# One pool of eight one-bank PSUM tiles for the last group of a DeltaNet and maxout kernel

## The chip, the cores and the metric

The kernel runs on one core of one Trainium2 chip. The metric is the time of one execution on the device, in microseconds (us); the time of a kernel is the median of several runs.

## The reference

The first half is a DeltaNet recurrence over 4 batches, 8 heads, 768 steps and 48 dimensions. The second half is a maxout layer on its 3,072 tokens, 384 wide, with 768 hidden units. All is float32.

```python
for t in range(S):
    y[:, :, t] = einsum('bhd,bhde->bhe', q[:, :, t], state)
    v_old = einsum('bhde,bhd->bhe', state, kt)
    state = state + bt[:, :, :, None] * einsum('bhd,bhe->bhde', kt, vt - v_old)
...
h = maximum(maximum(x @ w1, x @ w2), x @ w3)
out = h @ w_out
```

## The kernel before, in words

The sequence is cut into chunks of 64 steps, and two chunks of all batches make a group of 512 tokens; there are six groups. The order of all instructions is written out by hand: the loop at L1427 steps through the generator `ffn(m)`, which is the layer of group m, and between two of its yields issues pieces of the recurrence of group m + 1. The last group (m = 5) has no recurrence beside it, so from its first instruction on only the layer runs.

Every matmul writes into PSUM, which has eight banks. The pool `psum` (L76) hands them out under two tags. `ps_ffn` (L80) gives a tile of one bank and has 2 buffers. `ps_two` (L83) gives a tile of two banks and has 3 buffers, so the eight banks are all in use. When a tile is asked for and the buffers of its tag are all taken, the matmul that writes it waits until the reader of the buffer that comes free first is done.

The layer of the last group is worked out in two parts.

- **`crossed_hidden` (L1067)** makes the hidden values. Its two halves of 256 tokens, two of its three blocks of 128 inputs and pairs of 128 hidden units form a 2 by 2 by 2 block product, which is done with seven block products instead of eight (Strassen's scheme in Winograd's form), and the third block of inputs is added on top. Before the first product VectorE (DVE) makes four sums of the tokens, s1 to s4 (L1083 to L1086). Then come six units, for three pairs of hidden blocks and, for each, the second and the third weight (the first has been subtracted out of both, so the maximum is taken with zero and the first weight's part is added later). A unit has eight products, each in its own PSUM tile, `bank(0)` to `bank(7)`, and eleven matmuls of 128 by 256. Since a float32 matmul is two instructions on TensorE (PE), that is 22 per unit, 132 for the six. Products 0, 2, 3 and 4 are copied out of PSUM by ScalarE (ACT) into m1, m7, m5 and m6 (L1121, L1127, L1130, L1134). DVE makes four sums of these (L1135 to L1138) and adds the products 1, 5, 6 and 7 to them straight out of PSUM (`result`, L1108). In every second unit each of the four is followed by the maximum with the hidden values (L1110).
- **`outputs` (L947)**, used for the last two groups, makes the output in the same way. It takes two one-bank tiles, p and q, once, and uses them by turns: eleven products of twelve instructions of 128 by 192 each, 132 in all (L960). Its last instruction that reads PSUM is the DVE addition at L1042, which reads p; the addition at L1038 is the last that reads q. The helper `op` (L989) records all of these.

In `bank(n)` (L1114) the odd products take a `ps_ffn` tile and the even ones the first bank of a `ps_two` tile, whose second bank stays unused. So five products at most are in PSUM at once, three even and two odd. The tiles are named p_e and p_c in the profile, and those of `outputs` p_o.

Of the kernel before, what the change touches and what calls it, by code (L numbers as in the profile page):

```python
# [9 lines left out]
FP32 = mybir.dt.float32  # L10
# [13 lines left out]
def kernel(  # L24
# [42 lines left out]
    TOK = 512  # L67
# [5 lines left out]
    dram = ctx.enter_context(  # L73
        tc.tile_pool(name="dram", bufs=2, space=bass.MemoryType.DRAM)
    )
    psum = ctx.enter_context(  # L76
        tc.tile_pool(name="psum", bufs=1, space=bass.MemoryType.PSUM)
    )

    def ps_ffn(shape, name):  # L80
        return psum.tile(shape, FP32, name=name, tag="ffn", bufs=2)

    def ps_two(name):  # L83
        return psum.tile([128, 2, 512], FP32, name=name, tag="two", bufs=3)


    kpad = [const.tile([128, H, DP], FP32, name=f"kpad{i}") for i in range(4)]
# [21 lines left out]
    def rows(bb):  # L109
        return slice(C * bb, C * (bb + 1))  # L110
# [196 lines left out]
    def square(name):  # L307
        return work.tile([128, H, C], FP32, name=name, tag="square", bufs=17)
# [758 lines left out]
    def crossed_hidden(m, hs):  # L1067


        xt, vec = xts[m], nc.vector.tensor_tensor  # L1070
        plus = vec if m == GROUPS - 1 else nc.gpsimd.tensor_tensor
        lo, hi = slice(0, 256), slice(256, 512)
        a11, a12, a13 = (xt[:, t, lo] for t in range(KT))
        a21, a22, a23 = (xt[:, t, hi] for t in range(KT))
        spare = [t.rearrange("p a h d -> p (a h d)") for t in kmore]
        s1, s2, s3, s4 = (spare[0][:, 256 * n : 256 * (n + 1)] for n in range(4))
        parts = [
            work.tile([128, 2, HB * BL + HB], FP32, name=name, bufs=1).rearrange(
                "p s r -> p (s r)"
            )  # L1080
            for name in ("x_bl", "y_bl")
        ]
        vec(out=s3, in0=a11, in1=a21, op=ALU.subtract)  # L1083
        vec(out=s1, in0=a21, in1=a22, op=ALU.add)
        vec(out=s2, in0=s1, in1=a11, op=ALU.subtract)
        vec(out=s4, in0=a12, in1=s2, op=ALU.subtract)  # L1086
        for j in range(FT):
            hs[j] = square("h").rearrange("p h c -> p (h c)")
        for unit in range(2 * PAIRS):
            j, i = divmod(unit, 2)  # L1090
            w = {
                name: t[:, 128 * j : 128 * (j + 1)]
                for name, t in thirds[1 + i].items()
            }
            top, bottom = hs[j], hs[j + PAIRS]
            held = parts[unit % 2]
            m1, m5, m6, m7 = (held[:, 256 * n : 256 * (n + 1)] for n in range(4))
            c11 = spare[1][:, 256 * (unit // 2 % 2) :][:, 0:256]

            def times(to, *terms):  # L1100
                for n, (stays, moves) in enumerate(terms):
                    nc.tensor.matmul(  # L1102
                        to, w[stays], moves, start=(n == 0), stop=(n == len(terms) - 1)
                    )

            def result(h, base, p, spare=None):
                to = h if i == 0 else base if spare is None else spare
                vec(out=to, in0=base, in1=p, op=ALU.add)  # L1108
                if i:
                    nc.vector.scalar_tensor_tensor(  # L1110
                        out=h, in0=h, scalar=0.0, in1=to, op0=ALU.max, op1=ALU.max
                    )

            def bank(n):  # L1114
                return (ps_ffn([128, TOK], "p_e") if n % 2 else ps_two("p_c")[:, 0])[
                    :, 0:256
                ]

            p = bank(0)
            times(p, ("b11", a11))  # L1120
            nc.scalar.copy(m1, p)  # L1121
            p = bank(1)
            times(p, ("b21", a12), ("c1", a13))
            result(top[:, lo], m1, p, c11)
            p = bank(2)
            times(p, ("t3", s3))
            nc.scalar.copy(m7, p)  # L1127
            p = bank(3)
            times(p, ("t1", s1))
            nc.scalar.copy(m5, p)  # L1130
            yield
            p = bank(4)
            times(p, ("t2", s2))
            nc.scalar.copy(m6, p)  # L1134
            plus(out=m6, in0=m6, in1=m1, op=ALU.add)  # L1135
            plus(out=m1, in0=m6, in1=m5, op=ALU.add)
            plus(out=m7, in0=m7, in1=m6, op=ALU.add)
            plus(out=m5, in0=m5, in1=m7, op=ALU.add)  # L1138
            p = bank(5)
            times(p, ("c2", a13), ("b22", s4))  # L1140
            result(bottom[:, lo], m1, p)
            p = bank(6)
            times(p, ("t4", a22), ("c1", a23))
            result(top[:, hi], m7, p)
            p = bank(7)
            times(p, ("c2", a23))
            result(bottom[:, hi], m5, p)
            yield

    def ffn(m):  # L1150
        xt = xts[m]
        hs = {}

        def hidden(f, lo, w):
            if f not in hs:
                hs[f] = square("h").rearrange("p h c -> p (h c)")
            h = hs[f][:, lo : lo + w]
            for i in range(m > 0, 3):
                p_h = ps_ffn([128, TOK], "p_h")[:, 0:w]
                for t in range(KT):  # L1160
                    nc.tensor.matmul(  # L1161
                        p_h,
                        w_sb[i][:, t, f * 128 : (f + 1) * 128],
                        xt[:, t, lo : lo + w],
                        start=(t == 0),
                        stop=(t == KT - 1),
                    )
                if i == 0:
                    nc.scalar.copy(h, p_h)
                elif m and i == 1:  # L1170
                    nc.scalar.activation(  # L1171
                        out=h, in_=p_h, func=mybir.ActivationFunctionType.Relu
                    )
                else:
                    nc.vector.tensor_tensor(out=h, in0=h, in1=p_h, op=ALU.max)  # L1175
                yield


        early = FT // 2 if m == 0 else 0
        for lo in (0, TOK // 2):  # L1180
            for f in range(early):
                yield from hidden(f, lo, TOK // 2)
        if m >= GROUPS - 1:
            yield from crossed_hidden(m, hs)
            early = FT
        for f in range(early, FT):
            yield from hidden(f, 0, TOK)
        if m >= GROUPS - 2:
            yield from outputs(m, hs)
            return  # L1190
        for i in range(4):
            cc, g = divmod(i, 2)
            p_o = ps_ffn([128, DM], "p_o")
            last = slice(i * 128, (i + 1) * 128)
            terms = [(hs[f][:, last], wo_sb[:, f]) for f in range(FT)]
            if m:
                terms += [(xt[:, t, last], w_sb[0][:, t, 0:DM]) for t in range(KT)]
            for n, (stays, moves) in enumerate(terms):
                nc.tensor.matmul(  # L1199
                    p_o, stays, moves, start=(n == 0), stop=(n == len(terms) - 1)  # L1200
                )
                if m and n == 4:
                    yield
            o_sb = work.tile([128, DM], FP32, name="o_sb")
            nc.scalar.copy(o_sb, p_o)  # L1205
            for bb in range(2):
                tok0 = (2 * bb + g) * S + (2 * m + cc) * C
                nc.sync.dma_start(out=out[tok0 : tok0 + C, :], in_=o_sb[rows(bb)])
            yield
# [162 lines left out]
    CONVERTED = {*range(6), *range(11, 25)}  # L1372
    FETCHED = {8: 1, 12: 1, 13: 1, 14: 1, 18: 2, 19: 2, 20: 1, 21: 1}
    for i, _ in enumerate(ffn(0)):
        if i < 7:
            fetch(nc.sync if i else nc.gpsimd)
# [50 lines left out]
    for m in range(1, GROUPS):  # L1427
        for i, _ in enumerate(ffn(m)):
            if i == 0:
                some(solving, 3)  # L1430
            if m == 1 and i in (2, 5, 8):
                both_layers(i // 3)
            if m == GROUPS - 2 and i in (4, 5):
                cross_hidden(i - 3)
            if m == GROUPS - 2 and i in (8, 9):
                cross_weights(i - 8)
            if m + 2 < GROUPS:
                if i == 6:
                    blocks(m + 2)
                if i == 8:  # L1440
                    solving = solve(m + 2)
            links(m + 1, (LAST_LINKS if m == GROUPS - 2 else LINKS).get(i, ""))
            if i > 7:
                some(solving, 3 if i > 8 else 1)
# [29 lines left out]
```

## Time and profile before

| what | value |
|---|---|
| median of 3 runs | 512.43 us (511.62 to 514.18) |
| profiled execution: span from first to last instruction | 510.5 us |
| PE busy | 491.1 us, 96% of the span |
| DVE busy | 349.9 us, 69% |
| ACT busy | 168.7 us, 33% |
| first matmul of the last group's hidden values | 454.06 us after the span's start |
| first matmul of the last group's outputs | 484.60 us |
| last matmul of the outputs ends, by the chain of waits | 506.33 us |

The profiled execution's own time is not given apart from its span; the median of the runs is 512.43 - 510.5 = 1.9 us above that span.

The views used below: the timeline lists instructions in order of time (start, length, engine, line, operation, output<-inputs, how many were merged, and in square brackets how long the engine had been idle and who ended that). PE is the matmul, PEld the load of the matmul's weights, which runs ahead of it. A matmul's length in the timeline is a latency; matmuls overlap, and the distance between two starts is their rate. The chain of waits follows the work that ended last back to the start of the kernel.

### The profile page before, as it was taken

The numbers are of one execution on the slowest core, as the hardware profiler recorded it, in microseconds if no ns is written. First come the engines' busy times: TensorE is split into PE (matmuls) and PEld (weight loads), VectorE is DVE, ScalarE is ACT, GpSimd is POOL, SyncE is SP. The second block draws the span as 40 slices with busy tenths as digits, with TensorE's granted clock in tenths as the row PEclk, the third lists the DMA queues.
The fourth block names the chain that finished last, engine by engine and source line by source line (L and its number), as shares of the span: only waits on it lengthen the run. The fifth ranks groups of instructions, "written<-read, shape, count | busy, mean of one in ns | idle before, by whom it ended". The sixth has DMA issues, their size and how long they took to land.

```text
span 510.5 us, 18528 instructions
## 1 busy us (share of the span) xinstructions
PE 491.1 (96%) x8016; PEld 333.1 (65%) x8016; DVE 349.9 (69%) x801; ACT 168.7 (33%) x320; POOL 192.7 (38%) x317
## 2 busy tenths in 40 slices
PE   7778989999999999999999999999999999999996
PEld 6567778756565565665555565555655556998796
DVE  5897799969996430899563987635897455456752
ACT  5585664884422242210252101252101412113210
POOL 7434372783491926670575770503130000000000
PEclk9755999999999999999999999999999999999999
DMA  8938869764055925353675454923343202230001
GB/s 111 192 64 221 194 151 155 195 199 100 5 148 140 175 46 130 99 143 83 144 136 130 120 137 94 174 37 92 80 116 81 44 3 64 54 71 2 0 17 46
DMA packets 106304, 53.49 MB, mean 105 GB/s; under 512 B 89712, under 2 KB 99984, under 8 KB 106224
## 3 DMA queue, kind: packets, MB, share of 16 engines
q1 hardware_dynamic: 94352, 31.35, 30.4%
q0 software_dynamic: 9472, 20.37, 16.4%
q8 instruction: 63, 1.03, 0.9%
q10 hardware_dynamic: 2400, 0.59, 0.6%
q14 instruction: 17, 0.14, 0.1%
HBM read 39.17 MB, written 13.11 MB: 102 GB/s over the span
## 4 chain that ended last, share of the span: by engine, by line
PE 73%; DVE 14%; DMA 5%; ACT 4%; SPq 2%; issue 2%; POOL 0%; DVEq 0%; ACTq 0%; POOLq 0%
PE p_h L1161 26%; PE p_o L1199 13%; PE p_o L960 9%; PE p_e L1102 3%; DVE tmp L552 3%; PE p_g L406 3%; PE p_c L1102 2%; PE p_m L894 2%; PE p_u L759 2%; DMA kmore<-in_k_dram 2%; PE p_k L731 2%; PE p_y L801 2%; DVE y_bl L556 2%; PE p_s L782 2%; PE p_j L714 1%
## 5 line engine op out<-in xcount | busy, mean ns | idle before, releaser
L1161 PE MATMUL p_h<-xt,w_sb 128*128 128x512 f32 (+1 forms) x450 | 187.5, 558 | 0.7 <-ACT xt L827 0.6
L1161 PEld LDWEIGHTS p_h<-xt,w_sb 128*128 128x128 f32 x450 | 82.3, 193 | 68.7 <-issue 61.8
L1199 PE MATMUL p_o<-wo_sb,h 128*128 128x384 f32 x192 | 65.3, 490 | 0.0
L1175 DVE TENSOR_TENSOR h<-h,p_h 128x512 f32<-128x512 f32 (+1 forms) x42 | 25.4, 606 | 53.9 <-PE p_h L1161 52.8
L552 DVE TENSOR_TENSOR tmp<-x_bl,y_bl 128x31 f32<-128x31 f32 (+20 forms) x139 | 51.3, 369 | 4.1
L556 DVE TENSOR_TENSOR y_bl<-y_bl,tmp 128x31 f32<-128x31 f32 (+20 forms) x139 | 48.5, 349 | 4.8
L1199 PEld LDWEIGHTS p_o<-wo_sb,h 128*128 128x128 f32 x192 | 35.7, 190 | 23.2
L364 POOL DMA_DIRECT2D turned<-in_q_dram x72 | 39.1, 551 | 4.3 <-POOL turned L359 2.9
L1205 ACT COPY o_sb<-p_o 128x384 f32<-128x384 f32 x16 | 7.7, 479 | 85.8 <-PE p_o L1199 79.8
L1171 ACT ACTIVATE h<-p_h 128x512 f32<-128x512 f32 x24 | 14.3, 597 | 63.4 <-PE p_h L1161 60.5
L254 POOL TENSOR_TENSOR w_sb<-mant,up 128x384 int32<-128x384 int32 x18 | 19.1, 1059 | 39.3 <-DVE mant L250 39.2
L406 PEld LDWEIGHTS p_g<-kqt 48*64 48x64 f32 x1216 | 24.6, 142 | 9.0 <-issue 6.4
L406 PE MATMUL p_g<-kqt 48*64 48x64 f32 (+1 forms) x1216 | 27.8, 242 | 0.9 <-ACT kqt L335 0.8
L789 DVE TENSOR_TENSOR st<-st,p_s 48x768 f32<-48x768 f32 (+1 forms) x18 | 17.1, 949 | 15.4 <-PE p_s L782 15.2
L120 POOL DMA_DIRECT2D kpad<-in_k_dram x32 | 21.8, 690 | 14.1 <-issue 12.7
L1199 PE MATMUL p_o<-w_sb,xt 128*128 128x384 f32 x72 | 25.2, 486 | 0.0
L139 POOL DMA_DIRECT2D v_t<-in_v_dram x14 | 11.5, 829 | 35.5 <-PE p_u L759 35.5
L390 DVE TENSOR_TENSOR pt<-p_g,mask 128x512 f32<-128x512 f32 x20 | 13.8, 688 | 15.9 <-PE p_g L406 15.8
L287 POOL TENSOR_TENSOR v_t<-v_t,nrm 128x768 f32<-128x768 f32 x12 | 17.9, 1493 | 9.0 <-DVE nrm L281 8.9
L359 POOL MEMSET turned<- 128x96 f32 x18 | 3.3, 192 | 47.6 <-DVE kqt L380 47.6
L759 PEld LDWEIGHTS p_u<-v_t,ut 64*64 64x64 f32 x768 | 13.4, 141 | 10.1 <-issue 7.8
L1199 PEld LDWEIGHTS p_o<-w_sb,xt 128*128 128x128 f32 x72 | 13.7, 190 | 9.5
(212 smaller groups left out, 837.0 us busy)
## 6 DMA issues: line engine op xcount, KB each, us to landing
out_dram<-o_sb SPq DMA_DIRECT2D x40, 96.0 KB
w_bits<-in_moe_w_dram SPq DMA_DIRECT2D x9, 384.0 KB
w_bits<-in_moe_w_dram POOLq DMA_DIRECT2D x9, 384.0 KB, 5.2
turned<-in_q_dram POOLq DMA_DIRECT2D x72, 48.0 KB, 2.9
kpad<-in_k_dram POOLq DMA_DIRECT2D x32, 96.0 KB, 6.1
y_x<-y SPq DMA_DIRECT2D x16, 192.0 KB
qall<-y_x SPq DMA_DIRECT2D x32, 96.0 KB
v_t<-in_v_dram POOLq DMA_DIRECT2D x14, 192.0 KB, 5.0
```

Of the source, the lines that this page charges most:

```text
L120: queues[bb].dma_start(out=dst[rows(bb ^ g), :, 0:D], in_=src[2 * bb + g, :, c * C : (c + 1) * C, :].rearrange("h p d -> p h d"),)
L254: nc.gpsimd.tensor_tensor(out=dst.bitcast(I32), in0=mant_v.bitcast(I32), in1=up_v, op=ALU.add)
L364: (queue, nc.gpsimd)[i].dma_start(out=t[p0 : p0 + 32, bb, at : at + NP * 2 * D].rearrange("p (j x) -> p j x", j=NP), in_=(k, q)[i][2 * bb ...
L406: nc.tensor.matmul(p_g[rows(bb ^ (g * i)), par, c0 : c0 + C * (1 + whole)], kq[:, 0], kq if whole else kq[:, i],)
L552: nc.vector.tensor_tensor(out=t_v, in0=row.to_broadcast(t_v.shape), in1=column.to_broadcast(t_v.shape), op=ALU.mult,)
L556: nc.vector.tensor_tensor(out=rest, in0=rest, in1=t_v, op=ALU.subtract)
L759: nc.tensor.matmul(p_v[rows(bb ^ g), g, i], ut[c % NU][rows(bb), g, h], rhs[rows(bb), g, h],)
L960: nc.tensor.matmul(to[:, g], a[j][:, 128 * g : 128 * (g + 1)], b[j], start=(start and g == j == 0), stop=(stop and g == 1 and j == PAIRS - 1),
L1102: nc.tensor.matmul(to, w[stays], moves, start=(n == 0), stop=(n == len(terms) - 1))
L1161: nc.tensor.matmul(p_h, w_sb[i][:, t, f * 128 : (f + 1) * 128], xt[:, t, lo : lo + w], start=(t == 0), stop=(t == KT - 1),)
L1175: nc.vector.tensor_tensor(out=h, in0=h, in1=p_h, op=ALU.max)
L1199: nc.tensor.matmul(p_o, stays, moves, start=(n == 0), stop=(n == len(terms) - 1))
```

## The change

The pool is put in a stack of contexts of its own. Where the last group's layer begins, the pool is closed and another one, `banks`, is opened in its place. From then on `ps_ffn` has 8 buffers of one bank, nothing asks for a two-bank tile any more, and `bank(n)` takes a `ps_ffn` tile for every n. The two tiles of the last `outputs` come from the new pool too. `psum_pool` closes the old pool before it opens the new one; no argument says how the second pool waits for the first. No matmul, copy or addition is added, removed or reordered.

```diff
-    psum = ctx.enter_context(
-        tc.tile_pool(name="psum", bufs=1, space=bass.MemoryType.PSUM)
-    )
+    banks = ctx.enter_context(ExitStack())
+    pools = []
+
+    def psum_pool(name):
+        banks.close()
+        pools.append(
+            banks.enter_context(
+                tc.tile_pool(name=name, bufs=1, space=bass.MemoryType.PSUM)
+            )
+        )
+
+    psum_pool("psum")
 
     def ps_ffn(shape, name):
-        return psum.tile(shape, FP32, name=name, tag="ffn", bufs=2)
+
+        one = len(pools) > 1
+        return pools[-1].tile(shape, FP32, name=name, tag="ffn", bufs=8 if one else 2)
 
     def ps_two(name):
-        return psum.tile([128, 2, 512], FP32, name=name, tag="two", bufs=3)
+        return pools[-1].tile([128, 2, 512], FP32, name=name, tag="two", bufs=3)
...
             def bank(n):
-                return (ps_ffn([128, TOK], "p_e") if n % 2 else ps_two("p_c")[:, 0])[
-                    :, 0:256
-                ]
+                return ps_ffn([128, TOK], "p_e" if n % 2 else "p_c")[:, 0:256]
...
         if m >= GROUPS - 1:
+            psum_pool("banks")
             yield from crossed_hidden(m, hs)
```

## The prediction

> **What bounds the kernel now.** I read the page first, then the chain of waits, then the timeline of PE and DVE through the last group, then what PE and its weight loads waited for in that stretch.
>
> The page says which engine matters. Its columns are busy us, share of the span, instructions.
>
> ```profile
> span 510.5 us, 18528 instructions
> PE 491.1 (96%) x8016; PEld 333.1 (65%) x8016; DVE 349.9 (69%) x801; ACT 168.7 (33%) x320; POOL 192.7 (38%) x317
> ```
>
> PE is busy 96% of the span. The change touches only the last group: the hidden products from 454.06 us and the outputs from 484.60 us. There the chain of waits runs almost wholly through PE, and its end reads:
>
> ```profile
> 484.22 0.34 DVE y_bl L1108
> 484.56 0.04 issue
> 484.60 21.73 PE p_o L960 x132
> 506.33 0.02 issue
> 506.36 0.55 DVE up L989
> ```
>
> The 132 instructions of the outputs run in one piece of 21.73 us, 0.165 us each, with no step to another engine between. So whatever moves the first p_o matmul at 484.60 moves the end by the same amount, and the tail after it (the last addition and the stores, 506.36 to 510.5) moves along. The question is only when that matmul starts.
>
> What PE waits for between 453.9 and 484.7 is short:
>
> ```profile
> PEld p_e L1102 <- DVE y_bl L1108: 1.5, 4, 0.4
> PEld p_e L1102 <- DVE h L1108: 1.0, 3, 0.4
> PEld p_o L960 <- DVE y_bl L1108: 0.7, 1, 0.7
> ```
>
> Columns are total us, times, longest. All eight waits are for a DVE addition that reads a one-bank tile, and all eight stand before a matmul that writes one: seven p_e and the first p_o. Not one is before a p_c. They are waits for a bank and not for data: the second product takes only tokens (a12, a13) and weights, and it is the one that waits at 464.31, 469.52, 474.46 and 479.67. In the last unit this is how it looks:
>
> ```profile
> 479.16 0.59 PE L1102 MATMUL p_c<-xt,w_sb 128*128 128x256 f32 x2
> 479.67 1.13 PE L1102 MATMUL p_e<-xt,w_sb 128*128 128x256 f32 x4
> 480.64 0.59 PE L1102 MATMUL p_c<-kmore,crossed 128*128 128x256 f32 x2
> ...
> 483.23 0.59 PE L1102 MATMUL p_c<-xt,w_sb 128*128 128x256 f32 x2
> 483.66 0.59 PE L1102 MATMUL p_e<-xt,w_sb 128*128 128x256 f32 x2
> 484.60 2.22 PE L960 MATMUL p_o<-wo_sb,h 128*128 128x192 f32 x12 [0.34 <-DVE y_bl L1108]
> ```
>
> The reader should look at the starts. A pair (one float32 matmul of 128 by 256) follows another after 0.43 us. From 479.16 to 479.67 it is 0.51, and from 483.66 to 484.60 it is 0.94.
>
> **The change part by part.**
>
> *Eight buffers in place of three and two: the stalls inside the hidden products.* The free pitch is taken from unit 2 of 6, which has no stall: its first p_c starts at 459.05, the next unit's at 463.80, so eleven pairs take 4.75 us, 0.432 us a pair. The six units start at 454.06, 459.05, 463.80, 469.01, 473.95 and 479.16, and the pair after the sixth would start at 483.66 + 0.43 = 484.10. That makes 4.99, 4.75, 5.21, 4.94, 5.21 and 4.94 us, together 30.04. Six units without a stall take 6 x 4.75 = 28.50. The stalls cost 1.54 us: seven of them at 0.2 to 0.3 us. In each, 0.1 us is a restart: after a wait the next pair follows 0.53 us later (456.79 to 457.32) and not 0.43, because the weights could not be loaded ahead.
>
> With eight buffers a bank comes round after a whole unit. I checked the tightest one, product 5, the first that DVE adds after its four sums. In unit 4, which starts at 469.01, it is read from 473.99 to 474.40; unit 5 starts at 473.95 and writes its product 5 after six pairs, at 473.95 + 6 x 0.432 = 476.5. That leaves 2.1 us. Products 6 (read until 475.2, written again after eight pairs, at 477.4) and 7 (476.0 and 478.3) leave a little more. If PE runs 0.2 to 0.5 us faster a unit, as it then would, this cover shrinks by that at most. Nor does DVE fall behind over several units: in the six units it is busy 22.8 us of 30.4, by the table of stretches, which is 80% of the 28.5 that would be left. So I count all 1.54 us as **gained**.
>
> *The first output tile.* p of the last group is now the first `ps_ffn` tile to come free, and it waits until the addition of product 5 of the last unit ends, at 484.14 + 0.41 = 484.55. Its data, the upper hidden values of the left 256 tokens, have been done since 481.8. Of eight banks one has been free for us. The first p_o can follow at 484.10 in place of 484.60, and without the restart (24 instructions take 484.60 to 488.61, 4.01 us, where 24 at the pitch of 0.1625, from 492.51 to 494.46, take 3.90). **Gain 0.50 + 0.11 = 0.61 us.** What is late next: the second output product needs product 5's last maximum, which ends at 484.58 + 0.42 = 485.0, 5.84 us after the unit's start; PE would ask for it 4.75 + 1.95 = 6.70 us after the unit's start. It is hidden, by 0.86 us. The sums that DVE makes for the third and fourth products end at 488.6, 9.4 us after the unit's start, and are asked for at 10.6. They are hidden too.
>
> *The handover between the pools.* This is the one thing that is added, and the trace of before shows no pool that follows another, so it is bounded from both sides. The change writes no option for how the new pool reuses the old one's banks; the language's default is to wait for the old pool as a whole, that is for its last reader. That reader is the addition at L1042 of the group before:
>
> ```profile
> 452.31 0.55 DVE L989 TENSOR_TENSOR up<-up,p_o 128x384 f32<-128x384 f32 x1 [1.10 <-PE p_o L960]
> 454.26 0.55 DVE L989 TENSOR_TENSOR up<-up,p_o 128x384 f32<-128x384 f32 x1 [1.40 <-PE p_o L960]
> 454.73 0.42 DVE L1083 TENSOR_TENSOR kmore<-xt 128x256 f32<-128x256 f32 x1
> ```
>
> It waits for the last p_o itself and ends at 454.26 + 0.55 = 454.81. Now the first p_c does not wait for it, since it has another bank, and starts at 454.06. After a DVE read ends PE restarts 0.06 us later (456.73 to 456.79), so the first product would start at 454.87: 0.81 us later, and 0.10 for the restart. **Upper end 0.91 us lost.** Lower end: if each bank is waited for by itself, only the product that gets p's old bank waits. On the second product (now 454.49) that costs 0.38 + 0.10 = 0.48, on a later one nothing. So 0 to 0.91; I take 0.91, since a pool boundary is what the change writes. Behind the waiting matmul stand only PE's own products; ACT's first copy and DVE's first addition wait for those anyway. DVE's four sums (454.73 to 456.41) do not wait and are done before the third and fifth products need them at about 456.3 and 457.1. No DMA is moved, and no queue is passed.
>
> *The sum against the profiled execution.* -1.54 - 0.61 + 0.91 = -1.24 us. The span goes from 510.5 to 509.3 us. The runs' median stands 1.9 us above the span, so the median goes from 512.43 to **511.2 us**, 0.24% less.
>
> *A rule against the change.* PE would be idle for 0.8 us once, and the clock granted to it matters. In the stretch from 65 to 70 us PE is busy 4.07 of 5.00 us and the granted clock is 1.00; it is 1.00 in every stretch of the last group, with its seven short waits. The Trainium skill, page "TensorE: Matmul & The Clock Gate", section "A second HAM failure mode: psum-queue depth-cycling", describes a kernel in which cycling through PSUM banks leaves PE idle briefly so often that its clock falls back to half and recovers, over and over. By that rule one fall of the page's 3.4 us at half clock would cost some 1.7 us, an estimate, and the sum would be about +0.5 us. The rows here show no such fall, and the change takes short waits away.
>
> **The rivals.**
>
> 1. *The handover is paid bank by bank.* Then it costs 0 to 0.48 us and the sum is -1.7 to -2.15 us: 510.3 to 510.7. For it: in the kernel before, a tile waits only for its own buffer, as the p_e at 454.49, which does not wait for L1042. Against it: that is within one pool.
> 2. *The change doesn't do what it says: the stalls stay, because DVE's lateness and not the number of banks makes them.* Then only the first p_o is gained: -0.61 + 0.91 = +0.3 us, 512.7; with half the stalls gone -0.5, 512.0. For it: DVE reads product 7 of a unit up to 2.5 us after the unit's end. Against it: the cover of 2.1 us above.
> 3. *Slower: the handover waits for more than the readers of PSUM*, at the same place, in front of the first product. If it waited until the last stores of the group before had landed: the last of them is issued on ACT's queue at 454.84, and the kernel's own last store takes from 506.94 to the span's end at 510.5, 3.6 us; so the first product would start at 458.4, a loss of 4.3 + 0.1, and the sum is +2.3 us: 514.7. It decides as soon as the first product starts later than 454.06 + 2.15 - 0.1 = 456.1. For it: nothing in the trace; against it: those stores do not touch PSUM.
>
> **How the numbers follow.** Forecast, pool-wide handover at L1042 and all stalls gone: 0.64, at 511.2. Rival 1: 0.14. Rival 2: 0.14. Rival 3: 0.08. The range takes in rival 1 below and rival 2 above, and a few tenths for the medians, whose three runs spread from 511.62 to 514.18: 510.1 to 512.9. What a measurement of this kernel can tell from no change is about 0.5%, 2.6 us, and no case but the far end of rival 3, or the medians' own spread, leaves that band: faster 0.04, same 0.90, slower 0.06.
>
> **What the profile after would show.** The first p_c starts at about 454.87, released by DVE L989, with all later p_c at a pitch of 4.75 us a unit and no wait of a p_e for DVE L1108. The first p_o starts at about 483.4 and waits for nothing, and the outputs still take 21.7 us in one piece. The prediction is wrong if the first p_c starts at 454.06 (rival 1) or after 456.1 (rival 3), if p_c or p_e still wait for L1108 (rival 2), or if the second output product waits for DVE L1110.

## The result and the profile after

The changed kernel takes 511.21 us (median of 9 runs, 510.07 to 512.05) against 513.22 us for the kernel before, timed beside it (median of 9, 511.62 to 514.18). The ratio is 0.9955, with a 95% interval of 0.9935 to 0.9975: faster by 0.45%, which is inside the 0.5% that the prediction took as the least that can be told from no change. The profiled execution has a span of 510.2 us and took 512.05 us in all, the slowest of its nine.

So there are two things to explain: where the predicted 1.24 us went, and why the ratio says some 2.3 us. The profile answers the first. This is what PE's weight loads waited for from 452.9 to 485 us after the change, in place of the three lines of before:

```profile
PEld p_c L1113 <- DVE up L1000: 0.9, 1, 0.9
```

The seven waits of a p_e and the one of the first p_o are gone, and one wait is new: the first p_c waits for the addition that L1042 was before (now recorded at L1000). The timeline of the handover, PE first, then DVE:

```profile
454.27 0.81 PE L971 MATMUL p_o<-w_sb,xt 128*128 128x192 f32 x4
455.74 0.70 PE L1113 MATMUL p_c<-xt,w_sb 128*128 128x256 f32 x2 [0.65 <-DVE up L1000]
456.27 1.03 PE L1113 MATMUL p_e<-xt,w_sb 128*128 128x256 f32 x4
```

```profile
453.18 0.56 DVE L1000 TENSOR_TENSOR up<-up,p_o 128x384 f32<-128x384 f32 x1 [0.73 <-PE p_o L971]
455.13 0.56 DVE L1000 TENSOR_TENSOR up<-up,p_o 128x384 f32<-128x384 f32 x1 [1.40 <-PE p_o L971]
455.60 0.42 DVE L1094 TENSOR_TENSOR kmore<-xt 128x256 f32<-128x256 f32 x1
```

The addition ends at 455.13 + 0.56 = 455.69 and PE starts 0.05 us later; the pair after it follows at 0.53 and not 0.43 (455.74 to 456.27). And this is the other end of the hidden products:

```profile
483.47 0.59 PE L1113 MATMUL p_c<-xt,w_sb 128*128 128x256 f32 x2
483.90 0.59 PE L1113 MATMUL p_e<-xt,w_sb 128*128 128x256 f32 x2
484.33 4.06 PE L971 MATMUL p_o<-wo_sb,h 128*128 128x192 f32 x24
488.23 1.95 PE L971 MATMUL p_o<-w_sb,xt 128*128 128x192 f32 x11
```

The first p_o follows the last p_e at the free pitch, with no idle time in brackets, and its 24 instructions take 3.90 us.

To compare kernels whose earlier part runs early or late, I count a **last stage**: from the start of DVE's addition of L1042 in the last group but one (the last reader of the old pool) to the start of the very last addition. Before it is 454.26 to 506.36, 52.10 us; after it is 455.13 to 505.98, 50.85 us. The difference is -1.25 us.

What comes ahead of that stage was 0.87 us later in the changed kernel's profile (455.13 against 454.26), which is why the two spans differ by 0.3 us only. The instructions ahead of it are the same in both kernels, engine by engine, and in the same order but for two places near 32 and 39 us, where neighbouring matmuls change places within 0.1 us. The second profile of the kernel before (experiment 1) has them in the order of the changed kernel.

### The profile page after: what moved, and what is told of

It is laid out like the page before. It is cut to its first block, busy times and chain, and to the rows that moved or that the text cites. A ratio compares the mean times of both kernels' runs of the same rounds, so it can differ in the third digit from the quotient of the medians.

```text
span 510.2 us, 18525 instructions
## 1 busy us (share of the span) xinstructions
PE 489.5 (96%) x8016; PEld 333.6 (65%) x8016; DVE 349.8 (69%) x801; ACT 168.8 (33%) x320; POOL 192.7 (38%) x317
## 4 chain that ended last, share of the span: by engine, by line
PE 77%; DVE 7%; DMA 6%; ACT 4%; SPq 3%; issue 2%; POOL 0%; DVEq 0%; ACTq 0%; POOLq 0%
PE p_h L1170 28%; PE p_o L1209 17%; PE p_o L971 8%; PE p_e L1113 3%; PE p_c L1113 3%; PE p_u L770 2%; PE p_g L417 2%; PE p_m L905 2%; DMA qall<-in_q_dram 2%; PE p_s L793 2%; DMA kmore<-in_k_dram 2%; PE p_y L812 2%; SPq L131 2%; PE p_k L742 2%; PE p_j L725 2%
```

## The experiments

All eight are read by their last stage, in one table; the four that were timed (12 runs each) have a ratio to the kernel before, all to the same 35 runs of it on the same chip. The other four ran once, so only their last stage is read.

| kernel | L1042 starts at | last stage | expected | ratio (95%) |
|---|---|---|---|---|
| before | 454.26 | 52.10 | | |
| before, built again | 456.49 | 52.11 | 52.1 | 0.9993 (0.9969 to 1.0016) |
| after | 455.13 | 50.85 | 50.86 | 0.9955 (0.9935 to 0.9975) |
| after, built again | 455.07 | 50.86 | 50.85 | 0.9978 (0.9955 to 1.0001) |
| after, reuse tile by tile | 457.00 | 49.94 | 49.95 | 0.9979 (0.9952 to 1.0006) |
| before, tags swapped | 452.30 | 49.96 | 49.95 | 0.9960 (0.9935 to 0.9985) |
| second pool alone | 451.27 | 52.97 | 53.0 | |
| after, 5 buffers | 461.15 | 50.85 | 50.85 | |
| after, 4 buffers | 455.09 | 51.79 | 51.9 | |
| outputs' tiles alone | 456.38 | 51.50 | 51.5 | |

**1. The kernel before, built again.** No edit that reaches the program (a constant 2 is written as 1 + 1).

> The kernel before, built once more with nothing changed in its program, timed against itself. The last stage is counted from the start of the addition of L1042 of the last group but one to the start of the very last addition; it is 52.10 us in the profile of before (454.26 to 506.36) and 50.85 us after the change (455.13 to 505.98). Theory A (the change is worth only what stands in the last stage, -1.25 us; the rest of the measured ratio of 0.9955 is scatter of the first 450 us): last stage 52.1 us, and a ratio within 0.997 to 1.003. Theory B (a second pool also makes the program before the last group faster by some 1 us): the same ratio of 1.000 within 0.001, since scatter between two identical programs should be small.

The last stage is 52.11 us and the ratio 0.9993, with an interval 0.47% wide. Both theories expected that ratio, so it does not part them. But L1042 starts 2.23 us later in this profile than in the first, though it is the same program: between single executions, what comes ahead of the last stage scatters by more than the change is worth.

**2. The changed kernel, built again.**

> The changed kernel once more, with nothing else changed. Theory A: last stage 50.85 us, and the ratio to before nearer to 1 than at first: 0.9976 (510.5 us less 1.24), with scatter 0.995 to 1.000. Theory B: last stage 50.85 us too, and a ratio of 0.9955 again, within 0.001.

The last stage is 50.86 us, and the ratio moves to 0.9978, that is -1.1 us, with 1.24 us (0.9976) well inside. Theory B expected 0.9955 within 0.001 and got 0.9978. The first ratio's interval ended at 0.9975, just short of the 0.9976 that the stage explains; the second one contains it. It also has 0.9955 at its lower end, so the ratio leans to theory A and does not exclude B.

**3. The handover taken away.** The second pool reuses the banks tile by tile.

```diff
-                tc.tile_pool(name=name, bufs=1, space=bass.MemoryType.PSUM)
+                tc.tile_pool(
+                    name=name, bufs=1, space=bass.MemoryType.PSUM, reuse_waits="tile"
+                )
```

> The changed kernel, but the second pool takes the first one's banks tile by tile: a new tile waits only for the readers of the old tile that had its bank. The first product then has q's old bank, whose reader ended 2 us earlier. Theory A: the 0.91 us of the handover go as well, the first product starts about 0.2 us before the addition of L1042 as in the kernel before, last stage 52.10 - 2.15 = 49.95 us, 0.9 us less than after the change. Rival (part of the wait comes from somewhere else than the pool as a whole, such as the sums s1 to s4 being ready late): last stage 50.3 to 50.85 us.

The last stage is 49.94 us, 0.91 us less than after the change. PE waits for nothing that the profile shows between 455 and 486 us. The first product starts before the addition that it waited for:

```profile
454.85 2.11 PE L973 MATMUL p_o<-w_sb,xt 128*128 128x192 f32 x12
456.80 0.59 PE L1115 MATMUL p_c<-xt,w_sb 128*128 128x256 f32 x2
457.23 1.03 PE L1115 MATMUL p_e<-xt,w_sb 128*128 128x256 f32 x4
```

```profile
457.00 0.55 DVE L1002 TENSOR_TENSOR up<-up,p_o 128x384 f32<-128x384 f32 x1 [1.40 <-PE p_o L973]
```

456.80 is 0.20 us ahead of the addition at 457.00, as 454.06 was ahead of 454.26 before. The sums s1 to s4 delay nothing: the third product starts at 458.09, 0.86 us after the two pairs of the second. The ratio, 0.9979, does not show the gain of the stage: it is no better than the changed kernel's two, which says how coarse the ratios are.

**4. One pool, the two tags swapped.** One line of the kernel before:

```diff
-                return (ps_ffn([128, TOK], "p_e") if n % 2 else ps_two("p_c")[:, 0])[
+                return (ps_two("p_c")[:, 0] if n % 2 else ps_ffn([128, TOK], "p_e"))[
```

> The kernel before with one pool and the same five buffers, only the tags swapped: the odd products take the first bank of a two-bank tile (3 buffers), the even ones a one-bank tile (2 buffers). If the stalls came from too few banks (five of eight in use), they should stay: last stage about 52.1 us. Theory A refined (what stalled was the tag with two buffers, three of whose four products are read late by DVE; the even products are copied out by ACT at once, but for product 6): replayed by hand with the durations of the profile, no product waits, no handover is paid and p finds a free bank: last stage 49.95 us, 2.15 us less than before, 0.9 less than after the change.

The last stage is 49.96 us: all eight waits go with the same five buffers, and there is no handover to pay. Its profile has the shortest span of the four timed experiments, 506.5 us, but only 0.9 us of what separates it from the changed kernel's 510.2 lies in the last stage; the other 2.8 us lie ahead of it (452.30 against 455.13). The ratio is 0.9960 (0.9935 to 0.9985), better than the kernel before; against the changed kernel the intervals overlap.

**5. The second pool alone**, with the old buffers and the old use of them.

```diff
-        one = len(pools) > 1
-        return pools[-1].tile(shape, FP32, name=name, tag="ffn", bufs=8 if one else 2)
+        return pools[-1].tile(shape, FP32, name=name, tag="ffn", bufs=2)
...
-                return ps_ffn([128, TOK], "p_e" if n % 2 else "p_c")[:, 0:256]
+                return (ps_ffn([128, TOK], "p_e") if n % 2 else ps_two("p_c")[:, 0])[
+                    :, 0:256
+                ]
```

> The second pool alone: it is opened where the change opens it, but with the buffers of before (two of one bank, three of two banks) and the old use of them. Theory: the handover costs 0.91 us and all eight bank waits stay: last stage 52.10 + 0.91 = 53.0 us. Rival (the later start lets the readers catch up, and hides some of the handover): 52.1 to 52.8 us.

The last stage is 52.97 us, +0.87. All old waits are there beside the new one:

```profile
PEld p_e L1112 <- DVE y_bl L1118: 1.5, 4, 0.4
PEld p_e L1112 <- DVE h L1118: 1.0, 3, 0.3
PEld p_c L1112 <- DVE up L999: 0.9, 1, 0.9
PEld p_o L970 <- DVE y_bl L1118: 0.8, 1, 0.8
```

Of the rival's hiding there is at most 0.04 us. The span of this one profile is 508.4 us, 2.1 us less than the first profile of before, though its last stage is the longest of all: a span alone would have told the opposite.

**6. Five shared buffers**, and **7. four**: `bufs=8 if one else 2` becomes `bufs=5 if one else 2`, and 4.

> The changed kernel with 5 one-bank buffers in the second pool in place of 8, as many as were in use before, but shared by all products. Theory (it is the split into two tags that stalled, not the number): replayed by hand, five shared buffers never run out: last stage 50.85 us, as with eight. Rival (the number counts): the stalls stay, last stage 52.10 + 0.91 = 53.0 us, or something between.

> The changed kernel with 4 one-bank buffers. Theory: replayed by hand, one stall of 0.2 us in each unit from the second on, 1.0 us in all, and the first output tile still finds a free bank: last stage about 51.9 us. If nothing stalls: 50.85 us; if the stalls of before come back in full: 53.0 us.

Five give 50.85 us, the same as eight, and no wait but the handover. Four give 51.79 us, 0.94 more: five stalls of 0.19 us, one in each unit after the first, and none before the first p_o. The weight loads' waits with four:

```profile
PEld p_e L1113 <- DVE h L1119: 1.0, 3, 0.3
PEld p_c L1113 <- DVE up L1000: 0.9, 1, 0.9
PEld p_e L1113 <- DVE y_bl L1119: 0.6, 2, 0.3
```

From eight banks to five the number did not matter, the split did (with four it does): with two tags of three and two buffers PE waited for one tag while the other had a free bank.

**8. Only the outputs' tiles.** In the kernel before, p and q of the last group take the first bank of two two-bank tiles.

```diff
-        p, q = (ps_ffn([128, 2, HALF], "p_o") for _ in range(2))
+        if m < GROUPS - 1:
+            p, q = (ps_ffn([128, 2, HALF], "p_o") for _ in range(2))
+        else:
+            p, q = (
+                ps_two("p_o")[:, 0, 0 : 2 * HALF].rearrange("p (g x) -> p g x", g=2)
+                for _ in range(2)
+            )
```

> The kernel before with one pool, only the two output tiles of the last group take two-bank tiles (of which they use the first bank) in place of one-bank tiles. Theory: the first p_o finds a bank that ScalarE has long copied out; of the 2.15 us only the 0.61 at the first output go, the seven stalls inside the units stay: last stage 51.5 us, and no wait in front of p_o. If the first p_o waits for data and not for the bank: 52.1 us.

The last stage is 51.50 us, -0.60. The seven stalls stay, with the same totals of 1.5 and 1.0 us, and the wait before p_o is gone.

## Why the prediction was right

**The stalls inside the hidden products (1.54 us).** From the first p_c to the first p_o PE now takes 484.33 - 455.74 = 28.59 us, that is the 28.50 of six free units and the 0.1 of one restart. Before it was 484.10 - 454.06 = 30.04 up to the point where the first p_o could have followed. All seven stalls went. DVE did not become the bound, and rival 2 is refuted.

**The first output tile (0.61 us).** Experiment 8, which does this alone, gives 0.60 us.

**The handover (0.91 us).** Predicted was the first p_c 0.61 us after the start of L1042's addition (454.87 - 454.26), and a restart of 0.10; measured is 455.74 - 455.13 = 0.61, and 0.10. Experiment 3, which takes it away, gives 0.91 us, and experiment 5, which does it alone, 0.87. The new pool waited for the last reader of the old pool as a whole, so rival 1 does not hold for this change; nor did it wait for the stores, the last of which is issued at 455.71, so rival 3 does not hold either.

**The sum (-1.24 us).** The last stage shrank by 1.25 us. The pieces add up on the chip as they did on paper: 52.10 - 2.15 = 49.95 (experiments 3 and 4: 49.94 and 49.96), and 0.91 more is 50.86 (after: 50.85).

**The median.** The predicted 511.2 us was met by 511.21, and this is partly luck. The kernel before, timed again beside it, had a median of 513.22 and not 512.43, so the measured gain is larger than the predicted one: 2.3 us by the ratio, with an interval from 1.3 to 3.3. The second measurement of the change gives 1.1 us. So ratios of one change differ by as much as the rest of some 1 us, and I take the rest for scatter; no run shows what made it up in the first measurement. In the profiles the scatter lies ahead of the first matmul of the second group's weight product (p_m, L894 of the kernel before): over the ten profiles it starts between 165.6 and 175.6 us, while from it to L1042 all ten take 285.5 to 286.4 us, and the last stage repeats within 0.02 us for one program. Nor does a second pool bring an earlier p_m: in the six profiles with one it starts between 165.6 and 175.6 us, in the four without between 166.1 and 170.6.

**The rule against the change.** The page "TensorE: Matmul & The Clock Gate" (section "A second HAM failure mode: psum-queue depth-cycling") of the Trainium skill describes a clock that falls when PE idles briefly, and often, between products. The granted clock of the changed kernel around the handover is 1.00 (columns: stretch, length, then PE, PEld, DVE, ACT and POOL busy, granted clock, DMA share, GB/s):

```profile
455.00:460.00 5.00, 4.35 (x21) 3.77 (x21) 3.43 (x9) 1.49 (x4) 0.00 (x0) 1.00 0.32 79
460.00:470.00 10.00, 10.00 (x48) 8.81 (x47) 8.13 (x22) 2.98 (x8) 0.00 (x0) 1.00 0.00 1
```

The single idle time of 0.65 us was followed by no lower clock, here and in the four other profiles that have the handover, nor were the eight short waits of before, spread over 30 us. Whether more frequent ones would be, no run here shows.

What the prediction did not see is that the second pool is not needed: it counted what eight buffers remove and did not ask how many are enough. That the split made the waits was in the lines it showed, since all eight stood before a p_e or p_o of the two-buffer tag and none before a p_c.

## What to carry to other kernels

When matmuls wait for a PSUM bank, look which tag waits before adding buffers: here it was enough to give the products that a busy engine reads late the tag with more buffers, or to let all share one tag. Closing one pool and opening another over its banks cost the wait for the last reader of the whole old pool (0.91 us here), and nothing when the reuse was asked for tile by tile. And for a gain of 1 us in 510, compare a stretch of the profile that is free of the scatter, from one fixed instruction to another; here it repeated within 0.02 us where medians moved by 1 us.

## What the runs showed of the hardware that was not expected

In the profiles where the scatter of the first 170 us is largest, it goes with the granted clock. With five buffers, whose program is the same as the others' up to the last group, p_m starts at 175.6 us, the latest of the ten, and the span is 516.2 us. Between 125 and 130 us PE is idle for 2.7 us in one wait, and after it the clock is lower:

```profile
120.00:125.00 5.00, 5.00 (x58) 2.44 (x51) 3.72 (x13) 2.13 (x5) 0.94 (x1) 1.00 0.11 21
125.00:130.00 5.00, 2.30 (x64) 1.23 (x66) 4.83 (x13) 1.54 (x3) 2.35 (x4) 1.00 0.24 80
130.00:135.00 5.00, 5.00 (x147) 4.24 (x139) 4.83 (x12) 1.57 (x3) 1.45 (x2) 0.52 0.01 3
135.00:140.00 5.00, 5.00 (x76) 2.80 (x75) 4.97 (x7) 3.23 (x6) 2.54 (x3) 0.79 0.02 3
```

The granted clock is 0.52 and 0.79 in the ten microseconds after, where it stays at 1.00 in the nine other profiles. Beside the wait itself, these two rows stand for 0.48 x 5 + 0.21 x 5 = 3.45 us of PE's full-speed time. That the wait brought the clock down was not tried, and neither was why it came in that one execution. The length of a wait alone does not tell: between 60 and 75 us the clock is below 1.00 in four of the ten profiles, and PE's longest wait between 58 and 68 us is 1.00, 1.73, 1.75 and 2.46 us in these four, and 0.94 to 1.27 us in the six others.

The two profiles with the earliest p_m, the swapped tags (166.1 us) and the second pool alone (165.6 us), are also the two in which the clock has begun to rise between 45 and 50 us. In the other eight it is 0.50 there. In this order, swapped tags, second pool alone, after:

```profile
45.00:50.00 5.00, 4.58 (x114) 3.57 (x118) 4.55 (x16) 2.57 (x6) 0.54 (x1) 0.64 0.88 236
45.00:50.00 5.00, 5.00 (x137) 3.89 (x137) 4.30 (x15) 2.51 (x5) 0.56 (x1) 0.75 0.79 183
45.00:50.00 5.00, 4.80 (x78) 3.79 (x82) 4.45 (x16) 1.96 (x5) 0.32 (x1) 0.50 0.93 234
```

So the lead of the swapped tags ahead of the last stage, and the short span of the second pool alone, go with an earlier rise of the clock, 400 us before anything that these edits touch. What sets the moment of that rise was not tried.
